# Attention and expert layer on one core: the first block's scores moved ahead, and one step's weight loads made to wait

## The chip, the core and the metric

The kernel runs on one core of one Trainium2 chip. The metric is device microseconds of one execution; the median of three runs before the change is 530.3 us (529.27 to 530.62). The engines go by their names in the profile: PE is TensorE (PEld its weight loads), DVE is VectorE, ACT is ScalarE, POOL is GpSimd, SP is SyncE, which issues most transfers.

## The reference

Two layers follow each other. The first is attention over q, k, v of shape (4, 8, 768, 64): 4 batches, 8 heads, 768 positions, 64 wide. A position sees the 96 positions up to itself and the first 8 of its batch; a distance bias with a slope per head is added, then come softmax and the product with v.

```python
scores = scale * np.matmul(q, k.transpose(0, 1, 3, 2)) + bias
scores = np.where(is_global | is_local, scores, -1e9)
a = softmax(scores); x = (a @ v)            # rows of x: 3072 x 512
```

The second is a layer of 8 experts on the 3072 rows of x. Each row goes to the expert with the largest logit (`x @ w_gate`), and takes the next free slot of that expert (at most 768, in the order of the rows). Each expert computes `relu(rows @ w1) @ w2` with w1 of 512 x 1024 and w2 of 1024 x 512, and the result, times the gate's probability, is the output row.

## The kernel before, in words

**Attention (`banded`).** The 3072 rows are 24 blocks of 128 positions. For block i, `load(i)` (L474) issues three loads of 256 KB on SP: q, k and v (tiles nat_q, nat_k, nat_v), each in pieces of 256 bytes. `prep_k(i)` and `prep_q(i)` turn K and Q on PE, four transposes each into one of the four banks bankA (L511), and copy them out with DVE (K, L524) and ACT (Q, L537). `scores(u)` and `maxima(u)`, where u counts half blocks of four heads, write the scores to two banks of bankA (PE, L564) and add the bias and take the maxima (DVE, L545); `exps(u)` is the exponential on ACT (L575); `transpose_p` turns the probabilities (PE, L593 and L600), `weigh` multiplies them with V (PE, L621 and L624). The loop over t (from L649 on) interleaves the steps of several blocks: in round t it issues the loads of block t + 2 and the window of V, turns the probabilities of block t - 1, prepares K and Q of block t + 1, and then writes the scores of block t. From the end of the setup on, the order on PE, ACT and DVE is the written order; inside the loop that of SP and POOL too.

The two first blocks are loaded ahead of the loop. There V of block 0 and all three loads of block 1 wait until K of block 0 has landed (L483 to L485). Ahead of the loop PE turns Q and K of block 0 and runs six filling matmuls (L74).

**The seam.** Each block of x is stored to a tensor in memory (xrows, L180, on SP) and its rows are routed: logits, expert, slot. The slots go to a table in memory by indirect writes of POOL (L293). Expert 0 starts before all is routed: its slots 0 to 255 are gathered early, and the numbers of the rows in its slots 256 to 511 are worked out from the last blocks (tile gif, L389); `xs[3]()` (L1046) gathers these two blocks of 128 rows from xrows by indirect reads on POOL (L362; the second of them is `got`). They can start when the last block of x (xr_last, L178, L180) has landed in memory. Then POOL writes the last three columns of the table (L293), SP reads the whole table back (tile raw, L840), PE turns it (`turn_slots`, L854, L855), and its row numbers (gi, L1103) drive the gathers of the next expert.

**The experts.** Per expert 8 blocks of 128 columns of w1 (f = 0 to 7), two to a step; there are 32 steps. `raw_weights` (L117) loads a step in four pieces of 256 KB on SP (L134): two of w1 into tiles wr (4 buffers), two of w2 into w2r (7 buffers). Each piece is later split into a high part (ACT, L147) and a rest (DVE, L148), for the products L982 (layer 1) and L990 to L992 (layer 2). Steps 0 to 2 are loaded and split during attention. Step 3 is fetched at L1034, ahead of the gather, and split at f = 2 and 3 of expert 0; step 4 is fetched at f = 2, and so on two steps ahead. Three loads of 512 KB of w2 (L1065) wait for the read of the table. In this stage the order on PE, ACT and DVE is the written one; that of SP and POOL is set by the planner, which goes by written order and by when it reckons that an instruction is ready, so a load may be issued far ahead of its place in the text.

Of the kernel before, what the change touches and what calls it, by code (L numbers as in the profile page):

```python
# [20 lines left out]
P = 128  # L21
# [6 lines left out]
def fused(ctx: ExitStack, tc, q, k, v, wg, w1, w2, out, n_global, n_local, cap):  # L28
    nc = tc.nc
    B, H, S, D = q.shape  # L30
# [33 lines left out]
    SYNC = mybir.DependencyInfo(mybir.DependencyClass.Sync, mybir.DependencyReason.DATA)  # L64
# [26 lines left out]
    for n in range(2):  # L91
        nc.scalar.dma_start(out=wg_sb[n * D:(n + 1) * D, :, n * ER:n * ER + E],
                            in_=wg.rearrange("(c n p) e -> n p c e", n=2, p=D)[n])
# [68 lines left out]
    NBLK = N // P  # L162
    xts, rss = {}, {}
    PREFETCH = 3
# [6 lines left out]
    def store_rows(i):  # L171
        xt = xts[i // 3]
        xr_ps = bankA([P, DM])
        for c in range(KC):
            nc.tensor.transpose(xr_ps[:, c * P:(c + 1) * P], xt[:, c, i % 3, :], ident)

        xr = rt.tile([P, DM], F32, name="xr_last", bufs=1) if i == NBLK - 1 else small.tile([P, DM], F32, name="xr")
        nc.vector.tensor_tensor(xr.rearrange("p (h d) -> p h d", h=H), xr_ps.rearrange("p (h d) -> p h d", h=H),  # L178
                                rss[i // 3][:, i % 3, :].unsqueeze(2).to_broadcast([P, H, D]), op=ALU.mult)
        nc.sync.dma_start(out=xrows[i * P:(i + 1) * P, :], in_=xr)  # L180
# [118 lines left out]
    first = {}  # L299
# [91 lines left out]
    def route_steps(i0, T):  # L391

        r = dict(i0=i0, T=T)
        early = i0 + T < NBLK - LATE
        r["by"] = nc.gpsimd if early else nc.vector

        def s(r, then=None):
            route_p(r)
            route_s(r, then)
            route_g(r)  # L400

        def write(r):
            for i in range(T):
                route_w(r, i)
            if i0 + T == NBLK - EARLIER:
                route_early()
            if i0 + T == NBLK - LATE:
                route_first()

        if i0 + T == NBLK:  # L410

            first["n"] = lambda ps: route_n(r, ps)
            first["s"] = lambda ps, meanwhile: s(r, lambda: route_at(r, ps, meanwhile))
            first["w"] = lambda was=first["w"]: was() + [route_w(r, 0)]
            steps = (route_z, route_l, route_m, route_f)
        elif early:
            steps = (route_z, route_l, route_m, route_f, route_n, route_p, route_s, route_g, write)
        else:
            then = (lambda: route_at(r)) if i0 >= NBLK - LATE else None
            steps = [route_z, route_l, route_m, route_f, route_n, lambda r: s(r, then)]  # L420
            if then:

                first["w"] = lambda: [route_w(r, i) for i in range(T)]
            else:
                steps.append(write)
        return [lambda f=f: f(r) for f in steps]


    def banded():
# [44 lines left out]
        def load(i):  # L474
            b, j = blocks[i]
            d = st_[i]
            for n, src in (("q", q), ("k", k), ("v", v)):
                d[n] = nat.tile([P, H * D], F32, name="nat_" + n, bufs=5 if n == "v" else 3)
                ld = nc.sync.dma_start(out=d[n].rearrange("p (h d) -> p h d", h=H),
                                       in_=src[b, :, j * P:(j + 1) * P, :].rearrange("h p d -> p h d"))  # L480

                if i == 0 and n == "k":
                    first["k"] = ld  # L483
                elif i == 1 or n == "v" and i == 0:
                    tc.add_manual_dep(ld.ins, first["k"].ins.name, SYNC)  # L485

        load(0)
        load(1)
# [6 lines left out]
        def load_window(i):  # L495

            b, j = blocks[i]
            d = st_[i]
            if j == 0:
                d["vg"] = vpool.tile([G, H * D], F32, name="vg")  # L500
                nc.sync.dma_start(out=d["vg"], in_=d["v"][0:G])
            else:
                d["vg"] = st_[i - 1]["vg"]
                d["v1"] = vpool.tile([PREV + G, H * D], F32, name="v1", bufs=3)
                nc.sync.dma_start(out=d["v1"][0:PREV], in_=st_[i - 1]["v"][P - PREV:P])
                nc.sync.dma_start(out=d["v1"][PREV:PREV + G], in_=d["vg"])
# [60 lines left out]
        def exps(u):  # L567
            un = units[u]
            w, sc = un["w"], un["sc"]
            i, half = divmod(u, 2)  # L570
            if half == 0:
                st_[i]["sm"] = small.tile([P, H], F32, name="sm", bufs=3)
            sm = st_[i]["sm"][:, 4 * half:4 * half + 4]
            for a in range(4):
                un["e"] = nc.scalar.activation(sc[:, a, 0:w], sc[:, a, 0:w], AF.Exp, bias=un["mx"][:, a:a + 1], scale=-1.0,  # L575
                                               accum_out=sm[:, a:a + 1])
# [50 lines left out]
        def keep_x(i, by=None):  # L627
            if i % 3 == 0:
                xts[i // 3] = small.tile([P, KC, 3, P], F32, name="xt")
            if by is None:  # L630
                nc.scalar.copy(xts[i // 3][:, :, i % 3, :], st_[i]["xt_ps"])
            else:
                by.tensor_copy(xts[i // 3][:, :, i % 3, :], st_[i]["xt_ps"])
# [6 lines left out]
        def route(block, *steps):  # L640
            if block in groups:
                if block not in routes:
                    routes[block] = route_steps(*groups[block])
                for n in steps:
                    routes[block][n]()
# [3 lines left out]
        for t in range(NBLK + 1):  # L649
            x = t - 2  # L650
            rows = t > 1 and x < NBLK
            if t + 2 < NBLK:
                load(t + 2)
            if t < NBLK:
                load_window(t)
            route(t - 3, 1)
            if t < NBLK:
                route(t - 4, 3)
                route(t - 5, 7, 8)
            else:  # L660
                keep_x(x, nc.vector)
            if t > 0:
                transpose_p(2 * t - 2)
            if t == NBLK:
                store_rows(x)
            if t == NBLK - 1:
                route(t - 3, 2, 3)
            if rows and t < NBLK:
                keep_x(x)
            if t > 0:  # L670
                sums(t - 1)
            if t + 1 < NBLK:
                prep_k(t + 1)
                prep_q(t + 1)
            if t < NBLK - 1:
                route(t - 4, 4, 5)
            if t > 0:
                transpose_p(2 * t - 1)
            if t == NBLK:
                route(t - 4, 5, 6)  # L680
                start_rows()
                turn_first(0)
            if t == NBLK - 1:
                fetch_early()
                route(t - 3, 4)
            if rows and t < NBLK:
                store_rows(x)

            if t == 6:
                for n in range(PREFETCH):  # L690
                    pieces += raw_weights(n, nat, "wst", 4, loads=loads)
            if 6 <= t < 6 + len(loads):
                loads[t - 6]()
            if 8 <= t < 8 + len(pieces):
                pieces[t - 8](meanwhile=True)
            if t < NBLK:
                for u in (2 * t, 2 * t + 1):
                    scores(u)
                    maxima(u)
                exps(2 * t)  # L700
            route(x, 0)
            if t < NBLK:
                exps(2 * t + 1)
            if t > 0:
                weigh(2 * t - 2)
                weigh(2 * t - 1)
                turn_sums(t - 1)
            if t < NBLK:
                if t < NBLK - 1:
                    route(t - 3, 2)  # L710
                route(t - 4, 6)
            if t == 4:
                numbers()
# [299 lines left out]
    def plain(shape):  # L1013
        return moe.tile(shape, F32, name="w2r", bufs=7)

    def fetch(step, after=()):
        if step < STEPS and step not in wparts:
            pieces[step] = raw_weights(step, moe, "wr", 4, after, plain)
# [12 lines left out]
        if s.stop > SURE * P:  # L1031
            nc.scalar.activation(hr, h[:, SURE * P:], AF.Relu)  # L1032

    fetch(PREFETCH)  # L1034


    EARLY = 3
    START, LATER = slice(0, FIRST * P), slice(FIRST * P, T4)
# [5 lines left out]
        layer1(0, f, h_ps[f], xs[0], xs[1], START, (1,))  # L1044
    first["s"](y_ps[FIXED - 1], lambda: hidden(hs0, 0, START))
    got = xs[3]()  # L1046
    for w in first["w"]():
        tc.add_manual_dep(w.ins, got.ins.name, NOSYNC)
    hidden(hs0, 1, START)
# [13 lines left out]
    for step in range(PREFETCH):  # L1063
        t = wparts[step][1]["r"] = plain([P, FP, DM])
        ld = nc.sync.dma_start(out=t, in_=w2[0, step * FP * P:(step + 1) * FP * P, :].rearrange("(f p) d -> p f d", p=P))  # L1065
# [3 lines left out]
    for e in range(E):  # L1069
# [7 lines left out]
        for f in range(NF):  # L1077
# [11 lines left out]
            h = h_ps[f % 2]  # L1089
# [138 lines left out]
```

## Time and profile before

| | |
|---|---|
| median of the runs | 530.3 us (529.27 to 530.62) |
| profiled execution | 527.6 us, of it 525.8 us span |
| mean granted TensorE clock | 0.978 of full |
| PE busy | 488.0 us, 93% of the span |
| DVE busy | 313.2 us, 60% |
| ACT busy | 303.8 us, 58% |
| POOL busy | 130.0 us, 25% |
| DMA | 81.16 MB moved, mean 154 GB/s |

The times of the views below are microseconds from the span's start. In a row of the time-ordered view the first two numbers are the start and the duration; "x4" is the number of instructions merged in it, and the bracket at the end is how long the engine stood idle before it and what ended that. The attention loop runs to about 190 us, the seam from there to about 220 us, the experts from there on.

### The profile page before, as it was taken

To read this page: it belongs to the slowest core of one execution; us is meant where nothing else is said; L and a number is where in the kernel's file an instruction comes from. 1 tells how busy PE (TensorE), PEld (TensorE's weight loads), DVE (VectorE), ACT (ScalarE), POOL (GpSimd) and SP (SyncE) were. 2 spreads that over 40 slices of the span, in tenths; PEclk is the share of its full clock that TensorE was granted. 3 is DMA by queue.
4 is the path that set the end of the run, shared out by engine and by line. 5 is a ranking of instruction groups with operands and counts; after the bars stand their busy time and mean duration, and the time that the engine had idled before them with its cause. 6 is when DMAs were issued, how large, how long until landed. Compare 5 with 4: busy or idle time off the path is not lost.

```text
span 525.8 us, 10453 instructions
## 1 busy us (share of the span) xinstructions
PE 488.0 (93%) x3471; PEld 414.1 (79%) x3471; DVE 313.2 (60%) x945; ACT 303.8 (58%) x813; POOL 130.0 (25%) x222
## 2 busy tenths in 40 slices
PE   6999999999999975999999999999999999999860
PEld 3788888878888764878888889988989988888640
DVE  3777887877888854354546555654655554555320
ACT  1787788887988730344545555545555545546330
POOL 5111334435252322331311321311323103002020
PEclk9999999999999989999999999999999999999995
DMA  8987699989996216295535554563655355332010
GB/s 156 184 190 164 145 212 172 241 168 249 192 169 177 84 36 175 91 371 175 193 105 185 188 152 147 209 178 102 203 176 183 121 164 170 100 97 94 4 38 14
DMA packets 115936, 81.16 MB, mean 154 GB/s; under 512 B 81669, under 2 KB 98085, under 8 KB 115816
## 3 DMA queue, kind: packets, MB, share of 16 engines
q1 hardware_dynamic: 109240, 64.67, 48.2%
q0 software_dynamic: 5888, 14.71, 8.5%
q8 instruction: 88, 1.44, 1.2%
q14 instruction: 32, 0.26, 0.2%
q10 hardware_dynamic: 688, 0.07, 0.1%
HBM read 62.45 MB, written 14.75 MB: 147 GB/s over the span
## 4 chain that ended last, share of the span: by engine, by line
issue 52%; POOL 9%; POOLq 0%
POOL xg L362 5%; POOL out_dram L891 4%; POOL table L293 1%; POOLq L362 0%; POOLq L891 0%; POOLq L293 0%; POOLq L1155 0%
## 5 line engine op out<-in xcount | busy, mean ns | idle before, releaser
L575 ACT ACTIVATE sc<-sc,mx 128x232 f32<-128x232 f32 (+1 forms) x192 | 88.3, 462 | 26.2 <-DVE mx L545 16.8
L982 PE MATMUL bankB<-xh,w1h 128*128 128x416 f32 (+5 forms) x268 | 90.8, 344 | 2.1 <-ACT hr L1032 1.2
L982 PE MATMUL bankB<-xh,w1l 128*128 128x416 f32 (+5 forms) x268 | 89.8, 340 | 0.8 <-issue 0.8
L1029 ACT ACTIVATE hh<-bankB 128x512 fp32r<-128x512 f32 (+1 forms) x67 | 38.8, 580 | 86.8 <-PE bankB L982 80.6
L1030 DVE SCALAR_TENSOR_TENSOR hl<-bankB,hh 128x512 fp32r<-128x512 f32 (+1 forms) x67 | 44.6, 666 | 68.6 <-ACT hh L1029 64.3
L990 PE MATMUL bankA<-w2h,hh 128*128 128x512 f32 x192 | 79.3, 413 | 0.2 <-issue 0.2
L992 PE MATMUL bankA<-w2h,hl 128*128 128x512 f32 x192 | 76.2, 397 | 0.0
L991 PE MATMUL bankA<-w2l,hh 128*128 128x512 f32 x192 | 76.0, 396 | 0.0
L545 DVE CUSTOM_DVE_ANT_0 sc<-bankA,bias 128x232 f32<-128x232 f32 (+1 forms) x192 | 60.0, 377 | 9.4 <-PE bankA L564 9.1
L982 PEld LDWEIGHTS bankB<-xh,w1h 128*128 128x128 f32 x268 | 51.3, 191 | 10.4 <-issue 6.5
L982 PE MATMUL bankB<-xl,w1h 128*128 128x416 f32 (+5 forms) x268 | 57.4, 336 | 0.0
L362 POOL DMA_INDIRECT xg<-xrows,gi x28 | 28.6, 1020 | 111.7 <-PE bankC L347 102.3
L982 PEld LDWEIGHTS bankB<-xh,w1l 128*128 128x128 f32 x268 | 51.3, 192 | 4.1 <-issue 1.4
L148 DVE TENSOR_TENSOR w1l<-wr,w1h 128x512 fp32r<-128x512 f32 x58 | 37.5, 688 | 27.8 <-ACT w1h L147 23.0
L1032 ACT ACTIVATE hr<-bankB 128x256 f32<-128x256 f32 x64 | 24.6, 385 | 49.9 <-DVE hl L1030 44.5
L148 DVE TENSOR_TENSOR w2l<-w2r,w2h 128x512 fp32r<-128x512 f32 x58 | 37.4, 687 | 19.2 <-ACT w2h L147 17.3
L982 PEld LDWEIGHTS bankB<-xl,w1h 128*128 128x128 f32 x268 | 47.0, 188 | 0.7
L891 POOL DMA_INDIRECT out_dram<-ysb,to x16 | 16.0, 998 | 123.5 <-ACT ysb L883 121.1
L564 PE MATMUL bankA<-K,Q 64*128 64x232 f32 (+1 forms) x384 | 45.8, 366 | 0.2 <-DVE xr L178 0.2
L990 PEld LDWEIGHTS bankA<-w2h,hh 128*128 128x128 f32 x192 | 36.3, 189 | 10.3 <-issue 4.5
L992 PEld LDWEIGHTS bankA<-w2h,hl 128*128 128x128 f32 x192 | 36.2, 188 | 8.7
L564 PEld LDWEIGHTS bankA<-K,Q 64*128 64x128 f32 x384 | 36.9, 192 | 5.2 <-issue 3.0
(180 smaller groups left out, 858.9 us busy)
## 6 DMA issues: line engine op xcount, KB each, us to landing
wr<-in_moe_w_dram SPq DMA_DIRECT2D x58, 256.0 KB
w2r<-in_moe_w_dram SPq DMA_DIRECT2D x58, 256.0 KB
nat_q<-in_q_dram SPq DMA_DIRECT2D x24, 256.0 KB
nat_k<-in_k_dram SPq DMA_DIRECT2D x24, 256.0 KB
nat_v<-in_v_dram SPq DMA_DIRECT2D x24, 256.0 KB
xrows<-xr SPq DMA_DIRECT2D x23, 256.0 KB
v<-nat_v SPq DMA_DIRECT2D x20, 192.0 KB
wst<-in_moe_w_dram SPq DMA_DIRECT2D x12, 256.0 KB
```

Of the source, the lines that this page charges most:

```text
L148: (nc.gpsimd if meanwhile else nc.vector).tensor_tensor(parts["l"][:, s], r, parts["h"].bitcast(F32)[:, s], op=ALU.subtract)
L362: ld = nc.gpsimd.indirect_dma_start(out=xg, out_offset=None, in_=xrows[0:n], in_offset=bass.IndirectOffsetOnAxis(ap=gi.bitcast(U32), axis= ...
L545: nc.vector.tensor_tensor_reduce(out=un["sc"][:, a, 0:un["w"]], in0=un["ps"][hh][:, gg, :], in1=un["bias"][:, 4 * (u % 2) + a, :], scale=1 ...
L564: nc.tensor.matmul(pss[hh][:, gg, :], d["qt"][rows, g, :], keys[i // KT][rows, g, o + W - w:o + W], start=True, stop=True)
L575: un["e"] = nc.scalar.activation(sc[:, a, 0:w], sc[:, a, 0:w], AF.Exp, bias=un["mx"][:, a:a + 1], scale=-1.0, accum_out=sm[:, a:a + 1])
L891: w = nc.gpsimd.indirect_dma_start(out=out, out_offset=bass.IndirectOffsetOnAxis(ap=rows.bitcast(U32)[:, 0:1], axis=0), in_=ysb, in_offset ...
L982: nc.tensor.matmul(h_ps[:, s], ww[:, c, fs], xx[:, c, s], start=n == 0, stop=n == 3 * KC - 1)
L990: nc.tensor.matmul(y, hh[:, t], w2h[:, fi], start=f == 0, stop=False)
L991: nc.tensor.matmul(y, hh[:, t], w2l[:, fi], start=False, stop=False)
L992: nc.tensor.matmul(y, hl[:, t], w2h[:, fi], start=False, stop=f == NF - 1)
L1029: nc.scalar.activation(hh[:, s], h[:, s], AF.Relu)
L1030: nc.vector.scalar_tensor_tensor(hl[:, s], h[:, s], 0.0, hh.bitcast(F32)[:, s], op0=ALU.max, op1=ALU.subtract)
```

## The change

Two things are changed. In attention the loads of the two first blocks no longer wait for the first K, and in round 0 the transposes of block 1's K and Q stand behind the scores, maxima and first exponentials of block 0, ahead of its second exponentials; all later rounds are as before. At the seam the fetch of step 3's weights stands behind the gather, and each of its four loads waits until the second gathered block has landed. `fetch(step, after)` hands `after` to `raw_weights`, which adds a wait to each load.

```diff
             for n, src in (("q", q), ("k", k), ("v", v)):
                 d[n] = nat.tile([P, H * D], F32, name="nat_" + n, bufs=5 if n == "v" else 3)
-                ld = nc.sync.dma_start(out=d[n].rearrange("p (h d) -> p h d", h=H),
-                                       in_=src[b, :, j * P:(j + 1) * P, :].rearrange("h p d -> p h d"))
-
-                if i == 0 and n == "k":
-                    first["k"] = ld
-                elif i == 1 or n == "v" and i == 0:
-                    tc.add_manual_dep(ld.ins, first["k"].ins.name, SYNC)
+                nc.sync.dma_start(out=d[n].rearrange("p (h d) -> p h d", h=H),
+                                  in_=src[b, :, j * P:(j + 1) * P, :].rearrange("h p d -> p h d"))
...
-            if t + 1 < NBLK:
+            if 0 < t < NBLK - 1:
                 prep_k(t + 1)
                 prep_q(t + 1)
...
                 exps(2 * t)
+            if t == 0:
+
+                prep_k(1)
+                prep_q(1)
             route(x, 0)
...
-    fetch(PREFETCH)
-
...
     got = xs[3]()
+
+    fetch(PREFETCH, (got,))
     for w in first["w"]():
```

## Rows read from the trace of the kernel before

**Rows 1.** Busy time by stretches: stretch, its length, engines, PEclk, DMA share, GB/s.
```profile
57.00:168.00 111.00, 108.48 (x1165) 93.35 (x1161) 91.56 (x392) 93.37 (x321) 43.30 (x88) 1.00 0.94 198
213.00:500.00 287.00, 284.65 (x1482) 245.24 (x1481) 152.30 (x257) 150.33 (x297) 56.39 (x56) 1.00 0.48 156
```

**Rows 2.** In order of time, TensorE, the first 17 us.
```profile
5.48 0.66 PE L511 MATMUL bankA<-ident,nat_k 128*128 128x128 f32 x4 [0.41 <-DMA nat_k<-in_k_dram]
...
11.12 1.04 PE L511 MATMUL bankA<-ident,nat_k 128*128 128x128 f32 x4 [3.69 <-DMA nat_k<-in_k_dram]
...
12.94 1.97 PE L564 MATMUL bankA<-K,Q 64*128 64x128 f32 x16
...
16.40 0.60 PE L511 MATMUL bankA<-ident,nat_k 128*128 128x128 f32 x4
```

**Rows 3.** In order of time, SyncE's issues, the first load behind the wait.
```profile
5.45 0.37 SPq L479 DMA_DIRECT2D nat_v<-in_v_dram  x1
```

**Rows 4.** Busy time by stretches, the start.
```profile
5.00:6.50 1.50, 1.09 (x8) 0.78 (x8) 1.36 (x6) 0.60 (x1) 1.26 (x5) 1.00 0.00 0
...
11.50:14.50 3.00, 3.00 (x22) 2.67 (x22) 0.99 (x4) 0.60 (x1) 0.00 (x0) 0.50 1.38 218
```

**Rows 5.** In order of time, SyncE's issues around the seam.
```profile
185.55 0.33 SPq L180 DMA_DIRECT2D xrows<-xr  x1
...
196.21 0.38 SPq L325 DMA_DIRECT2D tbf<-table  x1
196.90 0.90 SPq L134 DMA_DIRECT2D wr<-in_moe_w_dram  x2
...
199.30 0.47 SPq L180 DMA_DIRECT2D xrows<-xr_last  x1
199.80 0.43 SPq L134 DMA_DIRECT2D wr<-in_moe_w_dram  x1
216.00 0.73 SPq L840 DMA_DIRECT2D raw<-table  x1
...
221.38 3.52 SPq L134 DMA_DIRECT2D w2r<-in_moe_w_dram  x6
```

**Rows 6.** In order of time, GpSimd around the seam.
```profile
190.39 0.98 POOL L293 DMA_INDIRECT table<-pay,slot_of  x1 [0.30 <-issue]
...
206.24 1.05 POOL L362 DMA_INDIRECT xg<-xrows,gif  x1 [14.87 <-issue]
207.60 1.01 POOL L362 DMA_INDIRECT xg<-xrows,gif  x1 [0.31 <-issue]
...
211.56 0.97 POOL L293 DMA_INDIRECT table<-pay,slot_of  x1 [0.30 <-issue]
```

**Rows 7.** In order of time, VectorE, TensorE and ScalarE at the seam.
```profile
197.28 0.68 DVE L178 TENSOR_TENSOR xr_last<-bankA,rs_last 128x512 f32<-128x512 f32 x1
...
200.27 0.16 DVE L389 TENSOR_TENSOR gif<-bankA,was 128x2 int32<-128x2 f32 x1
...
209.66 1.12 PE L347 MATMUL bankA<-ident,xg 128*128 128x128 f32 x4 [5.04 <-DMA xg<-xrows,gif]
...
218.92 0.21 DVE L850 CAST token<-raw 32x128 f32<-32x128 int32 x1 [1.43 <-DMA raw<-table]
...
219.39 0.25 PE L854 MATMUL bankC<-ident,token 32*128 32x32 f32 x1
...
220.79 1.13 ACT L147 CAST w1h<-wr 128x512 fp32r<-128x512 f32 x2
```

**Rows 8.** Busy time by stretches, around the seam.
```profile
186.00:187.50 1.50, 1.50 (x22) 0.92 (x22) 1.36 (x11) 1.25 (x3) 0.00 (x0) 1.00 0.46 175
192.50:195.50 3.00, 3.00 (x18) 2.90 (x18) 0.44 (x1) 0.01 (x1) 0.00 (x0) 0.50 0.00 0
198.50:204.50 6.00, 5.23 (x36) 4.03 (x34) 4.25 (x30) 0.98 (x3) 0.00 (x0) 1.00 0.95 299
```

**Rows 9.** In order of time, TensorE after the wait at the end of attention.
```profile
191.18 0.43 PE L196 MATMUL bankC<-xt,wg_sb 128*32 128x128 f32 x8 [1.31 <-issue]
```

## The prediction

> **What bounds the kernel now.** I read the busy table by stretches first. Between 57 and 168 us TensorE is busy 108.5 of 111 us at full clock, and between 213 and 500 us 284.7 of 287 us [rows 1]. So the body of both stages is a chain on TensorE, and time is to be had only where that engine stands still. The waits by engine and the time-ordered view then show two holes that belong to this change. The first is at the start: TensorE stands for 3.69 us until the second block's K has landed at 11.12 us, and the first block's scores, whose own K landed at 5.48 us, are queued behind those transposes and start at 12.94 us [rows 2]. The second is at the seam between attention and experts: 5.04 us until the gathered rows land at 209.66 us [rows 7], because the gather itself starts only at 206.24 us [rows 6], though its indices were ready at 200.43 us [rows 7]. The rest of the path moves along with these holes: what is gained there is gained at the end, if no other supply is late.
>
> **Part 1, the start: loads at once.** Before, V of the first block and all of the second wait for the first K: the next load after the first K is issued at 5.45 us, as that K lands [rows 3]. The DMA engines moved nothing between 5.0 and 6.5 us [rows 4]: that is the hole in the supply. Without the wait the stream runs on. Its rate for these loads is 218 GB/s [rows 4], so one load of 262 KB takes 1.2 us. Before, the stream restarts at about 6.6 us; the second block's K is its third load, 6.6 + 3.6 = 10.2 us, and it was seen at 11.12 us, 0.9 us after its data. After, the stream goes on from about 4.8 us, the end of the first K. The third block's K is the sixth load from there: 4.8 + 6 x 1.2 + 0.9 = 12.9 us. I take 12.8 us.
>
> **Part 2, the start: scores first.** Nothing is added or removed: sixteen matmuls go ahead of eight transposes on TensorE, and on ScalarE the second block's Q copy goes between the two halves of exponentials. TensorE is free at 11.12 - 3.69 = 7.43 us [rows 2], and the first block's scores can start there, 5.5 us earlier than 12.94. The moved transposes need the second block's K, by the same sum at 4.8 + 3.6 + 0.9 = 9.3 us, when the scores are nearly over; they fall into the time in which TensorE waits for exponentials, which is their cover. Without that cover they would cost their own 1.2 us (two groups of 0.6 us, by the row at 16.40 us [rows 2]). What is late next? Before, 16.40 - 12.94 = 3.46 us passed from the scores to the third block's transposes; after, that gives 7.43 + 3.46 = 10.9 us, with the moved transposes at most 12.1 us. The third K at 12.8 us is later than both. So the gain is read at the third block's transposes: 16.40 - 12.8 = 3.6 us. Bounds: 5.5 us, if the third K is in time; and 0.5 us, if the six loads are served in turn rather than one after the other, so that the first K lands at about 4.8 + 4.8 + 0.9 = 10.5 us and the scores start some 2 us (5.48 to 7.43 [rows 2]) later, at 12.5 us. I stay with 3.6 us, since the second K landed after barely more than its own three loads had moved although four more were issued behind it.
>
> The wait for the third K leaves TensorE idle for about 1 to 2 us near 11 to 12.8 us. [...] By the rows a slow stretch of 3.0 us does the work of 1.5 us, so with it the sum would be 1.5 us smaller; without it, as below. I leave it out of the sum, for the transposes of the probabilities lie inside this wait, and keep it in the range.
>
> **Part 3, the seam: step 3's weights wait.** Before, four loads of step 3 and two of step 4, 256 KB each, are issued from 196.90 to 199.80 us; the store of the last rows of x is issued at 199.30 us as the sixth of seven [rows 5], though its data were ready at 197.28 + 0.68 = 197.96 us [rows 7]. The seven moved together at 299 GB/s until about 204.5 us [rows 8], and the gather started 1.74 us after that [rows 6]. After, step 3's loads are queued behind the gather's landing. Step 4's take their buffers from the same ring of four after step 3's, so I expect them behind as well. The store then goes at about 198.05 us. An undisturbed store of the same size, issued at 185.55 us [rows 5], had moved its data by 187.5 us [rows 8], so 1.95 us. Gather start: 198.05 + 1.95 + 1.74 = 201.7 us, against 206.24: 4.5 us. It cannot be earlier than the indices, 200.43 us, which bounds the term at 5.8 us.
>
> From the gather's start to the first use there are 3.42 us (206.24 to 209.66), so the rows land at 205.1 us, and of the 5.04 us wait some 0.5 us are left. What is late next is the slot table: two gathers and three scatters run one after another on GpSimd (206.24 to 211.56 + 0.97 us [rows 6]), the table is read at 216.00 us [rows 5], 3.47 us after the last scatter, and VectorE has it at 218.92 us [rows 7]. That is 12.68 us from the gather's start, all of it carried along: 201.7 + 12.7 = 214.4 us. TensorE turns the table 0.47 us later (219.39 [rows 7]), so it cannot gain more than 4.5 us there, however early its rows were.
>
> What the new wait holds: SyncE issues in order, and behind step 3's loads stand step 4's and the read of the table. The second gather lands at about 201.7 + 1.36 + 3.42 = 206.5 us (it starts 207.60 - 206.24 = 1.36 us after the first [rows 6]); six loads are 1.57 MB, at 299 GB/s 5.3 us, so their data run from about 207.7 to 213 us. The table read, due at 211.5 us, can stand up to 1.5 us behind them; with only step 3's four loads (3.5 us, until 211.2) it would not. The scatters can be slower as well: the three that ended at 191.37 us were read only at 196.21 us, 4.84 us [rows 5, 6], against 3.47. I take 0.5 us off. The weights themselves: ScalarE converts the first of them at 220.79 us [rows 7], so at about 216.8 us after; they land by 214 us. That slack of 2.8 us hides the delayed load; beyond it every us is paid. So this part gives 4.0 us, bounds 2.6 (the scatter's 1.4 us more and 0.5) and 5.8.
>
> [...]
>
> **Sum.** 3.6 + 4.0 = 7.6 us. The profiled execution took 527.6 us, a span of 525.8 and 1.8 us around it: 520.0 us after. The median of the three runs is 530.3 us, 2.7 us above it, and the forecast is for such a median: 522.7 us.
>
> **Rivals.**
> (a) The head start is given back in the attention stage, because that is paced by DMA. For it: the engines' share is 0.94 between 57 and 168 us at 198 GB/s [rows 1]. Against it: the saturated stream at the start shows a share of 1.38 [rows 4], and TensorE idles only 2.5 us of the 111. Only the seam is left: 530.3 - 4.0 = 526.3 us.
> (b) The seam does not move: step 4's loads, which wait for nothing new, or others are issued ahead of the store, or the gather waits for something else (the trace puts its wait down to no single transfer for certain). 530.3 - 3.6 = 526.7 us.
> (c) Both: no change, 530.3 us.
> (d) Slower: the order on SyncE puts step 3's loads behind the table read, the three loads of 512 KB that follow it and six more of 256 KB. For it: in the old order the six are issued together behind the table read, at 221.38 us [rows 5]; against it: the gather lands before the scatters. Then 3.1 MB at 299 GB/s, 10.5 us, and 1.8 us for the first half of step 3 pass after the table at 214.9 us, and the first conversion starts at about 228 us instead of 216.8: 11.3 us late, 3.7 us more than is gained, 534.0 us. It decides from a landing after 216.8 + 7.6 = 224.4 us.
>
> **How the numbers follow.** Forecast 0.62; (a) 0.11; (b) 0.12; (c) 0.09; (d) 0.06. About 0.3%, 1.6 us, is what a measurement of this kernel can tell from no change. The forecast, (a) and (b) are faster: 0.85; same 0.09; slower 0.06. The forecast's own bounds: both upper terms nearly (5 and 5.5) give 519.8 us; lower terms (3.6 less 1.5, and 2.6) give 525.6 us. The range goes from 519.5 to 526.8 us, so that it takes in (a) and (b).
>
> **What would show it.** Right: the scores of the first block near 7.5 to 8 us; the third block's transposes near 12.8 us, waiting for K; no load of weights between 196 and 206 us (times of the seam as they stand above; the head start of 3.6 us comes off them as well); the store issued right behind its VectorE instruction; the gather 4 to 5 us closer to the indices; TensorE's wait for the rows under 1 us, and a small new one before the turning of the table. Wrong: the first K later than 7 us; a clock of 0.50 near 13 us; loads of step 4 ahead of the store; ScalarE standing before the first conversion of step 3; a difference at the seam's start that is not kept at 168 us.

## The result and the profile after

The changed kernel takes 525.38 us (median of 8 runs, 522.82 to 526.97) against 529.27 us for the kernel before in the same series: ratio 0.990, 95% interval 0.9875 to 0.9925. By the medians that is 3.9 us, by the ratio 5.3 us. The forecast was 522.7 us and 7.6 us: side and range are right, the gain is a third to a half smaller, and 522.7 / 530.3 = 0.986 lies outside the interval. On another chip the ratio was 0.992 (c_after below).

The profiled execution after took 526.28 us, with a span of 524.6 us (before: 527.6 and 525.8). TensorE is busy for 490.3 us of it, before for 488.0. Three views show the change. First the table by stretches (columns as in [rows 1]): from 11 to 13 us TensorE does next to nothing, from 13 to 16.5 us it runs at 0.53 of its full clock, and from 206 to 214 us the DMA engines are loading (share 0.63, 194 GB/s). The third line lies behind the last rows of x: there the clock is low as well, at 0.50, where it was at 1.00 before [rows 8].

```profile
11.00:13.00 2.00, 0.07 (x2) 0.04 (x1) 0.77 (x2) 1.73 (x9) 0.19 (x1) 1.00 1.36 217
13.00:16.50 3.50, 3.50 (x18) 3.08 (x20) 1.38 (x2) 0.60 (x1) 0.07 (x1) 0.53 1.34 222
198.50:204.20 5.70, 5.70 (x20) 5.02 (x21) 2.80 (x16) 0.38 (x1) 3.78 (x4) 0.50 0.31 92
206.00:214.00 8.00, 7.68 (x52) 6.59 (x50) 2.24 (x4) 2.99 (x7) 0.00 (x0) 1.00 0.63 194
```

Then the view in order of time: start, duration, engine, line and operation, in brackets the idle time before it and its releaser. The shifted line numbers: L506 turns K and Q, L559 is the scores, L839 the read of the slot table, L849 the token, L853 its turning.

```profile
7.95 1.16 PE L559 MATMUL bankA<-K,Q 64*128 64x128 f32 x16
...
12.99 0.92 PE L506 MATMUL bankA<-ident,nat_k 128*128 128x128 f32 x4 [1.93 <-DMA nat_k<-in_k_dram]
...
15.55 2.34 PE L559 MATMUL bankA<-K,Q 64*128 64x232 f32 x16
...
196.20 0.32 SPq L180 DMA_DIRECT2D xrows<-xr_last  x1
...
199.50 1.05 POOL L362 DMA_INDIRECT xg<-xrows,gif  x1 [9.70 <-DVE pay L283]
...
204.61 0.90 SPq L134 DMA_DIRECT2D wr<-in_moe_w_dram  x2
...
204.82 0.97 POOL L293 DMA_INDIRECT table<-pay,slot_of  x1 [0.30 <-issue]
...
205.36 0.60 PE L347 MATMUL bankA<-ident,xg 128*128 128x128 f32 x4
...
206.53 1.32 SPq L134 DMA_DIRECT2D wr<-in_moe_w_dram  x2
...
212.62 0.73 SPq L839 DMA_DIRECT2D raw<-table  x1
...
215.19 0.21 DVE L849 CAST token<-raw 32x128 f32<-32x128 int32 x1 [3.44 <-DMA raw<-table]
...
215.83 0.24 PE L853 MATMUL bankC<-ident,token 32*128 32x32 f32 x1 [2.14 <-DVE gate L851]
...
222.49 0.50 PE L989 MATMUL bankA<-w2h,hh 128*128 128x512 f32 x1 [1.81 <-ACT hr L1031]
```

Against [rows 2, 5 to 7]: the first scores start 5 us earlier, the third block's transposes 16.40 - 12.99 = 3.4 us. The store is issued right behind its data, the gather starts 6.7 us earlier, and TensorE's 5.04 us wait for the rows is gone. But the last table write ends at 204.82 + 0.97 = 205.79 us and the table is read only at 212.62 us: 6.83 us where it was 3.47. Into that gap fall the six loads, issued from 204.61 to 207.85 us. Two new waits of TensorE follow, 2.14 and 1.81 us.

The same milestones, read from the time-ordered view of every profile (starts in us; "write" is the end of the last table write, "last" the scores of the last block):

| profile | 2nd scores | 5th | last | xr_last | gather | write | raw | token | span |
|---|---|---|---|---|---|---|---|---|---|
| before | 18.03 | 39.26 | 179.51 | 197.28 | 206.24 | 212.53 | 216.00 | 218.92 | 525.8 |
| after | 15.55 | 37.22 | 177.96 | 195.49 | 199.50 | 205.79 | 212.62 | 215.19 | 524.6 |
| e_start | 14.57 | 35.74 | 174.40 | 189.30 | 199.81 | 206.10 | 209.54 | 212.02 | 520.6 |
| e_seam | 18.07 | 39.30 | 176.42 | 191.31 | 197.17 | 203.46 | 210.16 | 212.75 | 522.2 |
| e_late | 14.42 | 35.58 | 172.99 | 187.88 | 193.60 | 199.89 | 203.01 | 205.81 | 518.3 |
| e_warm | 14.64 | 35.80 | 174.77 | 189.66 | 195.03 | 201.31 | 208.14 | 211.51 | 521.7 |
| c_before | 17.24 | 38.46 | 176.31 | 192.60 | 202.13 | 208.41 | 211.57 | 214.15 | 522.0 |
| c_after | 15.77 | 37.24 | 177.10 | 194.25 | 198.26 | 204.56 | 211.08 | 213.29 | 520.7 |
| e_queue | 14.24 | 35.42 | 175.50 | 191.74 | 195.76 | 202.04 | 205.47 | 207.71 | 514.5 |
| e_behind | 15.42 | 36.99 | 177.14 | 195.66 | 199.67 | 205.97 | 209.84 | 212.34 | 519.7 |
| e_vlate | 12.59 | 34.15 | 173.93 | 190.21 | 194.22 | 200.51 | 206.66 | 208.91 | 518.0 |
| e_best | 12.64 | 33.81 | 174.97 | 192.14 | 196.16 | 202.46 | 206.15 | 208.31 | 518.0 |
| e_best2 | 13.27 | 34.44 | 174.04 | 190.27 | 194.86 | 201.13 | 205.02 | 207.26 | 516.0 |
| e_last | 12.85 | 34.02 | 172.89 | 189.98 | 194.54 | 200.83 | 204.29 | 206.92 | 513.5 |

The first two rows are from one chip, e_start to e_warm from a second, c_before to e_behind and e_last from a third, e_vlate to e_best2 from a fourth; absolute times are compared within a chip, differences within a profile across them.

### The profile page after: what moved, and what is told of

The parts are those of the page before. It is cut to its first block, busy times and chain, and to the rows that moved or that the text cites. A ratio compares the mean times of both kernels' runs of the same rounds, so it can differ in the third digit from the quotient of the medians.

```text
span 524.6 us, 10457 instructions
## 1 busy us (share of the span) xinstructions
PE 490.3 (93%) x3471; PEld 415.9 (79%) x3471; DVE 313.6 (60%) x945; ACT 304.1 (58%) x813; POOL 129.9 (25%) x222
## 4 chain that ended last, share of the span: by engine, by line
issue 51%; PE 24%; POOL 9%; DMA 7%; ACT 3%; SPq 2%; DVE 1%; POOLq 0%; DVEq 0%; ACTq 0%
PE bankA L559 6%; POOL xg L362 4%; DMA nat_k<-in_k_dram 4%; POOL out_dram L890 4%; PE bankB L588 4%; PE bankA L506 3%; PE bankC L616 3%; PE bankB L595 3%; PE bankC L619 3%; ACT sc L570 2%; DMA v<-vg 2%; SPq L479 1%; PE bankA L175 1%; DMA xg<-xrows,gi 1%; POOL table L293 1%
## 5 line engine op out<-in xcount | busy, mean ns | idle before, releaser
L559 PE MATMUL bankA<-K,Q 64*128 64x232 f32 (+1 forms) x384 | 46.1, 364 | 0.2
L559 PEld LDWEIGHTS bankA<-K,Q 64*128 64x128 f32 x384 | 36.5, 188 | 6.1 <-issue 3.4
```

The costliest lines, as they stand in the source:

```text
L559: nc.tensor.matmul(pss[hh][:, gg, :], d["qt"][rows, g, :], keys[i // KT][rows, g, o + W - w:o + W], start=True, stop=True)
```

## Experiments

**The parts alone, the loads behind the table, and a warm clock.** e_start has the start's part only, e_seam the seam's part only:

```
 e_start = after     +    fetch(PREFETCH)                # back ahead of EARLY = 3
                     -    fetch(PREFETCH, (got,))
 e_seam  = before    -    fetch(PREFETCH)
                     +    fetch(PREFETCH, (got,))        # behind got = xs[3]()
 e_late  = after     -    fetch(PREFETCH, (got,))
                     +    fetch(PREFETCH, (listed,))     # behind raw, listed = slots([got])
 e_warm  = after     +    if t == 1: busy(8)             # ahead of prep_k(2): eight dummy matmuls
```

> The start alone is changed; step 3's weights are fetched ahead of the gather as in the kernel before. Theory (the head start is cut to 1.8 us by the half clock between 13.0 and 16.5 us, and what is left is kept): third block's transposes near 13.0 us, the last rows of x (VectorE, xr_last) near 195.5 us against 197.28, the wait for the gathered rows again about 5 us, the time 1.8 us under the kernel before. Rival, the term as predicted: 3.6 us under it. Rival, attention is paced by DMA: xr_last at 197.3 us and no gain.

> The seam alone is changed; the start is that of the kernel before. Theory (the waiting weights delay the last scatter and TensorE's code, so that of the 4.9 us by which the gather moves some 1.9 us are left): xr_last at 197.3 us, gather start 4.0 us behind it, table on VectorE 19.7 us behind it against 21.6, time 1.9 us under the kernel before. Rival, the term as predicted: table 17.6 us behind it, time 4.0 us under.

> As the changed kernel, but step 3's weights wait until the slot table has been read, so that nothing is loaded beside the scatters and the table. Theory (those loads held the last scatter and TensorE's code back): table read 3.5 to 4 us after the last scatter against 6.8, table on VectorE 16.7 us behind xr_last against 19.7, the long branch of 4.9 us on TensorE under 3 us, time about 2 to 3 us under the changed kernel, if the later weights don't stop ScalarE at their first conversion (then less by that wait). Rival (the scatters land late for themselves, as the three ahead of the early table did, 4.8 us): table read 4.8 us or more after the last scatter, time within 1 us of the changed kernel.

> As the changed kernel, with eight filling matmuls on TensorE in its wait for the third block's K (11.0 to 13.0 us). Theory (half clock after that wait costs 1.6 us of the head start): granted clock 1.00 from 13.0 to 16.5 us, the second block's scores near 14.3 us against 15.55, xr_last 1.2 to 1.6 us earlier than 195.5, time 1.2 to 1.6 us under the changed kernel unless the seam eats it. Rival (the stretch is paced by VectorE and ScalarE): scores earlier, but xr_last at 195.5 us.

Measured against the kernel before (525.69 us): e_start 521.51 us, ratio 0.9913 [0.9888, 0.9939]; e_seam 522.60, 0.9941 [0.9913, 0.9969]; e_late 518.81, 0.9846 [0.9801, 0.9891]; e_warm 524.90, 0.9985 [0.9958, 1.0011]. In e_seam the read of the table, 6.70 us behind the last write, reproduces the delay without any change of the start:

```profile
202.37 0.90 SPq L134 DMA_DIRECT2D wr<-in_moe_w_dram  x2
...
202.49 0.97 POOL L293 DMA_INDIRECT table<-pay,slot_of  x1 [0.30 <-issue]
...
210.16 0.73 SPq L840 DMA_DIRECT2D raw<-table  x1
```

By the medians e_start is 4.2 us under the kernel before, nearer to its rival (3.6) than to its theory (1.8), and e_seam 3.1 us (theory 1.9, rival 4.0).

In e_late, where the loads are issued 2.8 us behind that read, it is 3.12 us, and VectorE has the token 17.9 us after xr_last instead of 19.7 (after), 21.4 (e_seam) or 21.9 (e_warm). A part of these distances comes from the store: in e_seam, e_late and e_warm SyncE issued it 2.1 to 2.4 us after xr_last, behind the read of an earlier table (tbf) that waits for table writes, against 0.71 us in the profile after, and the gather started 5.4 to 5.9 us after xr_last and not 4.0. So the token came later than was expected in e_seam (19.7) and e_late (16.7); with the old seam on this chip (e_start) it came 22.7 us after. The other half of the theory was a branch on TensorE's sequencer ahead of the turning of the table, which took 4.92 us after, from 210.9 to 215.8 us. In e_seam and e_warm, which have the late read too, TensorE's wait there (2.3 and 4.39 us) ended with VectorE's token, and in e_late none stands there; so in the two the read and not the branch set it.

What e_late gained is in part given back at once: ScalarE now waits for the weights, the last time 5.39 us. The two loads that this conversion needs were issued at 210.71 us, ahead of six loads of w2r and behind three of 512 KB, and were not there before 223.06 us.

```profile
198.92 0.97 POOL L293 DMA_INDIRECT table<-pay,slot_of  x1 [0.30 <-issue]
...
203.01 0.73 SPq L839 DMA_DIRECT2D raw<-table  x1
205.80 2.13 SPq L134 DMA_DIRECT2D wr<-in_moe_w_dram  x2
...
209.23 0.62 ACT L147 CAST w1h<-wr 128x512 fp32r<-128x512 f32 x1 [1.58 <-DMA wr<-in_moe_w_dram]
...
210.71 1.05 SPq L134 DMA_DIRECT2D wr<-in_moe_w_dram  x2
211.80 10.52 SPq L134 DMA_DIRECT2D w2r<-in_moe_w_dram  x6
...
223.06 1.36 ACT L147 CAST w1h<-wr 128x512 fp32r<-128x512 f32 x2 [5.39 <-DMA wr<-in_moe_w_dram]
```

The clock. e_start waits as long for the third K as the changed kernel does, 2.11 us, and yet its clock stays up: second scores at 14.57 us, 1.0 us earlier than after. e_warm fills the wait (0.39 us left) and the clock is at 1.00 from 13 to 16.5 us, but its fifth block is no earlier than e_start's. So beside e_start there was nothing to save, and e_warm is slower than e_start alone (its interval only touches that of e_seam). Its profile shows the same late read (6.83 us), a longer wait of TensorE for the token (4.39 us) and a mean clock of 0.66 from 210 to 220 us; but e_start has 0.68 from 200 to 210 us at the seam too. Why e_warm is that much slower stays open. The first two lines are e_start's, the others e_warm's:

```profile
13.14 0.63 PE L506 MATMUL bankA<-ident,nat_k 128*128 128x128 f32 x4 [2.11 <-DMA nat_k<-in_k_dram]
13.00:16.50 3.50, 3.36 (x31) 2.92 (x32) 2.12 (x7) 0.90 (x2) 0.10 (x1) 1.00 1.35 222
...
11.00:13.00 2.00, 1.82 (x9) 0.62 (x7) 0.79 (x2) 1.82 (x9) 0.09 (x1) 1.00 1.37 219
13.00:16.50 3.50, 3.29 (x30) 2.85 (x32) 2.06 (x7) 0.83 (x2) 0.16 (x1) 1.00 1.34 219
```

**Both kernels again, and two other places for the loads.** e_queue puts them behind the table's read in the queue without waiting until it has landed; e_behind puts them ahead of gather and writes:

```
 e_queue:  -    fetch(PREFETCH, (got,))
           +    fetch(PREFETCH, (listed,), NOSYNC)        # behind slots([got]); order only
 e_behind: -    fetch(PREFETCH, (got,))
           +    fetch(PREFETCH, (first["st"],), NOSYNC)   # order behind the store of xr_last
```

> The changed kernel itself, beside the next ones. Theory (the weights held back run beside the third scatter and hold it up): raw is read 6.5 to 7 us after the last scatter has ended, as in e_seam and e_warm, the token comes 21 to 22 us after xr_last, and the ratio to the kernel before is 0.990 to 0.995. Rival (the two parts simply add): 0.9913 of e_start and 0.9941 of e_seam multiply to 0.9855, raw is read 3.5 us after the last scatter.

> The kernel before, profiled on this chip: raw 3.5 us after the last scatter, the gather 8 to 9 us after xr_last, the token 21.6 us after it (all as in its first profile); time 525 to 529 us.

> As e_late, but step 3's loads stand right behind the read of the slot table in SyncE's queue and don't wait until it has landed (205.80 - 203.01 = 2.8 us earlier). If a transfer that is first in its queue keeps its place: the token comes 17.9 us after xr_last as in e_late, ScalarE's waits of 1.58 + 1.34 us for the weights go, and the ratio is 0.981 to 0.984. If loads hold up any small transfer near them, as they did the third scatter: the token comes 2 to 3.5 us later (20 to 21.4 after xr_last), and the ratio is 0.988 to 0.992.

> Step 3's and step 4's loads stand right behind the store of the last rows in SyncE's queue, ahead of gather and scatters; the store is as early as in the changed kernel. Six loads of 256 KB take 5.3 us at 299 GB/s, so they are done about 9.7 us after xr_last; the last scatter starts 11 us after it (e_late). If only what runs beside loads is late: gathered rows 2 to 3.4 us late (TensorE waits 2 to 5 us for them), the scatter not, raw 3.1 to 3.5 us after it, the token 18 to 19 us after xr_last, ratio 0.984 to 0.988. If the gather's delay is passed on through GpSimd's order: the token at 20 to 21.4 us, ratio 0.990 to 0.994, so no better than the changed kernel.

Against 525.78 us: c_after 521.06 us, 0.9920 [0.9888, 0.9952]; e_queue 518.26, 0.9872 [0.9826, 0.9919]; e_behind 519.58, 0.9888 [0.9836, 0.9941]; c_before's one profiled run took 523.79 us. The timings do not separate the three (their intervals overlap, and e_queue's ratio lies above its forecast of 0.981 to 0.984); the profiles do. Write to read: 3.16 us in c_before, 6.52 in c_after, 3.43 in e_queue, 3.87 in e_behind. xr_last to token: 21.6, 19.0, 16.0 and 16.7 us. In e_queue the loads stand 0.8 us behind the read and do not hold it up, so the harm is not done to any small transfer near them, but to the table write that goes out together with them:

```profile
201.07 0.97 POOL L293 DMA_INDIRECT table<-pay,slot_of  x1 [0.30 <-issue]
...
205.47 0.73 SPq L839 DMA_DIRECT2D raw<-table  x1
206.25 0.95 SPq L134 DMA_DIRECT2D wr<-in_moe_w_dram  x2
...
207.71 0.22 DVE L849 CAST token<-raw 32x128 f32<-32x128 int32 x1 [0.97 <-DMA raw<-table]
```

In e_behind it is the gather that runs beside the loads, and the rows come 204.97 - 199.67 = 5.30 us after its start instead of the 3.42 us of the kernel before [rows 6, 7]; the writes start when GpSimd has issued the gathers, so only TensorE waits, 1.97 us:

```profile
199.67 1.06 POOL L364 DMA_INDIRECT xg<-xrows,gif  x1 [10.70 <-DVE pay L285]
...
204.97 0.66 PE L349 MATMUL bankA<-ident,xg 128*128 128x128 f32 x4 [1.97 <-DMA xg<-xrows,gif]
...
209.84 0.73 SPq L841 DMA_DIRECT2D raw<-table  x1
```

c_after and e_behind fell to the low clock, 0.51 and 0.53, behind the wait for the third K, c_after thus:

```profile
13.00:16.50 3.50, 3.46 (x16) 3.11 (x18) 1.31 (x2) 0.60 (x1) 0.00 (x0) 0.51 1.35 221
```

e_queue, with the same start, did not (1.00 from 13 to 16.5 us, second scores at 14.24 against 15.77 us). With the profile after, e_start and e_late that makes three profiles of six in which the clock fell behind a wait of 1.8 to 2.1 us. What decides it was not found.

**The wait for the third K taken away, and the pieces put together.** e_vlate loads Q and K of the third block ahead of all V; e_best is that with e_queue; e_best2 also puts the read of an earlier table (tbf), which waits for table writes, behind the store of xr_last on SyncE; e_last also has five buffers for w2r:

```
 e_vlate: -  load(0); load(1)
          +  load(0, "qk"); load(1, "qk")
          +  # t == 0: load(2, "qk"), then V of blocks 0, 1 and 2
 e_best2: +  store_rows(NBLK - 1)
          +  first["read"]()              # tbf's load, with its old waits
 e_last:  -  name="w2r", bufs=7
          +  name="w2r", bufs=5
```

> The changed kernel with V of the first two blocks loaded behind Q and K of the third: the third K is the sixth load and not the eighth, 2 x 1.2 us earlier. If TensorE's wait for that K costs the head start: third K near 10.6 us instead of 12.8 to 13.0, no wait over 0.5 us before it, granted clock 1.00 throughout 10 to 20 us, scores of the second block at 12.2 to 12.8 us (14.2 at full clock, 15.4 to 15.8 at half clock in the runs so far), those of the fifth at 33.4 to 34 us (35.4 to 37.2 so far); seam as in the changed kernel (raw 6.5 us after the last scatter); ratio 0.985 to 0.990. If the stream of loads paces attention anyway: the wait comes back as one for V or for the fourth K, the fifth block's scores stay at 35.4 us or later, ratio 0.990 to 0.994.

> e_queue with the order of loads of e_vlate. If both causes are the right ones: start as in e_vlate, token 16 to 18 us after xr_last, ratio 0.979 to 0.984. If only the seam's: 0.985 to 0.988, as e_queue.

> e_best with the read of the first table queued behind the store of the last rows and not ahead of it. Where attention ends early, that read stands before the store and waits for the last table write (store 2.36 us after xr_last in e_late, 0.71 us in e_queue). If the store's place counts: 0.71 us in any case, and up to 1.6 us less than e_best where e_best shows a later store; otherwise the same as e_best within 1 us.

> e_best2 with five buffers and not seven for the second layer's raw weights, so that of the six loads that stand ahead of the fifth step's first-layer weights in SyncE's queue four come later. Theory (what was gained at the token is partly given back where ScalarE waits for those weights: 2.30 us in e_best2, 1.75 in e_best, 5.39 in e_late): the wait at the second pair of conversions goes, they start near 218 us instead of 220.5, and from the token to the end of the span there are 306 to 307 us instead of 308.7; ratio 0.979 to 0.983. Rival (TensorE has slack there, or fewer buffers make a later load late): 308 us or more from the token to the end, ratio 0.983 to 0.990.

Against 526.15 us: e_vlate 519.58 us, 0.9878 [0.9842, 0.9914]; e_best 519.38, 0.9863 [0.9832, 0.9894]; e_best2 517.40, 0.9843 [0.9798, 0.9888]. e_last, against 526.71 us: 517.07, 0.9816 [0.9774, 0.9858]. In e_vlate the wait is gone and the clock stays up; the one that comes in its place, for the fourth K, is 0.75 us:

```profile
10.44 0.60 PE L506 MATMUL bankA<-ident,nat_k 128*128 128x128 f32 x4
...
12.59 1.84 PE L559 MATMUL bankA<-K,Q 64*128 64x232 f32 x16
...
17.79 0.63 PE L506 MATMUL bankA<-ident,nat_k 128*128 128x128 f32 x4 [0.75 <-DMA nat_k<-in_k_dram]
```

The clock was 1.00 from 11 to 16.5 us in e_vlate and e_last; the second block's scores took 1.84 us in all four kernels with that order, as in e_warm at 1.00, against 2.34 us after, and their fifth block starts at 33.8 to 34.4 us. At the seam e_vlate still has the late read (6.15 us) and the other three don't (3.46 to 3.89). In time that can't be told apart here: e_best, with its token 16.2 us after xr_last instead of 18.7, stands at 0.9863 beside e_vlate's 0.9878, above the 0.979 to 0.984 that were expected if both causes count. So the late read is shown at the table, and what it is worth in the whole time is not. e_best2 could not show the store's place: the store is issued 0.7 us after xr_last in e_best as well, since attention ended late enough on that chip, and the 0.002 between the two is not explained.

In e_last there are 306.6 us from token to end as expected (e_best2: 308.7), but ScalarE's wait went only from 2.30 to 1.61 us. The expectation had taken the wrong loads for the ones that ScalarE waits for: those that moved forward, to 212.65 us (in e_best2 220.57), are the next step's and are converted at 230.53 us. The conversion that waits needs the pair before, issued at 209.94 us (in e_best2 210.21), ahead of the loads of w2r in both kernels. So the shorter time from token to end has another cause than the one given, or is within the scatter of single profiles:

```profile
209.94 1.57 SPq L134 DMA_DIRECT2D wr<-in_moe_w_dram  x2
...
212.65 2.35 SPq L134 DMA_DIRECT2D wr<-in_moe_w_dram  x2
...
219.93 1.39 ACT L147 CAST w1h<-wr 128x512 fp32r<-128x512 f32 x2 [1.61 <-DMA wr<-in_moe_w_dram]
...
230.53 1.13 ACT L147 CAST w1h<-wr 128x512 fp32r<-128x512 f32 x2
```

e_last is below the changed kernel: beside c_after on the same chip the intervals do not overlap. From e_best2, measured on another chip, it is not separated.

## Why the prediction was right in part

*Bounds and parts 1 and 2.* The holes were where the rows put them. First scores 7.95 us (forecast 7.5 to 8), third K 12.99 (12.8). The 3.6 us are there where the clock stays up: e_seam to e_start, one with the old start and one with the new, 39.30 - 35.74 = 3.56 us at the fifth block. Where it falls, 39.26 - 37.22 = 2.0 us are left. The sentence that failed is "I leave it out of the sum": the price was right (1.5 us; the fifth block at 37.0 to 37.2 against 35.4 to 35.8 us), but in three profiles of six it was paid. The reason given, that the transposes of the probabilities lie inside this wait, did not hold: they are done 1.9 us before the third K lands. The slow stretch that the 1.5 us were worked out from is that of 3.0 us at 0.50 [rows 4, 8], which came after waits of 3.69 and of 1.31 us [rows 2, 9]; that such a wait brings it was the author's estimate, and behind the wait for the third K the clock was at 0.51 to 0.53 in three profiles of six.

*Rival (a), the head start given back in attention.* A part of it, and on the third chip more. From the fifth to the last block the new start took 0.5 us more than the old one on the first chip (140.74 against 140.25), 0.3 to 1.9 on the second (e_start, e_late and e_warm against e_seam), 2.0 to 2.3 on the third (c_after, e_queue and e_behind against c_before), where c_after was only 1.2 us ahead at the fifth block and is 0.8 us behind c_before at the last. On the second chip the waits name DMA (1.7 us for K in e_start, 1.1 for V in e_warm); on the third they are waits for ScalarE. Against it: e_start is 4.2 us faster than the kernel before. With one profile of the old start on each chip I take the sign as likely and the size as open.

*Part 3, the seam.* Store, order on SyncE, gather and the vanished wait came as worked out: from xr_last to the gather 8.96 us before and 4.01 after, 4.95 us gained against 4.5 forecast (5.5 us in c_before and c_after). Step 4's loads did queue behind step 3's, and ScalarE did not wait for the weights. The step that failed is "I take 0.5 us off" for table writes beside loads: it measured 6.83 - 3.47 = 3.4 us (3.4 in c_after as well), and not as a queue ahead of the table's read, but in the last write: SyncE had issued its last load by 207.85 us and then waited 4.6 us for that write. With it the token gains not 4.0 us but 1.9 in its distance from xr_last (2.5 on the third chip). Of the terms that were read it is the largest of the miss, and e_late and e_queue, which take the loads away from the writes, have the token 17.9 and 16.0 us after xr_last, where the kernel before has 21.6 us in both of its profiles. None of the rows shows a table write beside such loads; the 1.5 us at most by which the read was to stand behind them were too few as well.

*Behind the token* the forecast let everything move along. In the profile after, token to end is 309.4 us against 306.9, so 2.5 us are lost there, 1.81 of them in the wait at 222.49 us; in c_after it is 307.4 against 307.8. What makes this wait is open: it is put down to ScalarE's hr, and stands in no other profile; the branch on TensorE's sequencer before it took 4.69 us and ended 1.3 us before the wait did, which was not tested. It is not all of it, since e_seam and e_warm, without that wait, have 309.5 and 310.2 us.

The forecast had no clock at the seam, and there it fell too. From xr_last to the token TensorE is busy 17.32 of 19.70 us after and 15.69 of 21.64 before, so it stands 3.6 us less; but the granted clock of that stretch is 0.83 against 0.92. That makes some 3.4 against 1.7 us of work not done, by my estimate (0.17 x 19.70 and 0.08 x 21.64 us). In c_after and c_before it is the other way: 0.75 from 190 to 198 us and 0.97 from 200 to 212 us, against 1.00 and 0.72, by time 0.88 against 0.83 in the mean. So of the seam's gain in the profile after about 1.6 us went to the clock, and a single pair of profiles does not show whether the change is to blame.

*Open too:* the parts' ratios multiply to 0.9855, the changed kernel stands at 0.990 and 0.992. The delayed write is in e_seam already, so it doesn't explain the difference; the intervals allow additivity only at their edges, and the whole was not timed on the chip of the parts. The two profiles differ by 1.3 us in time where the medians differ by 3.9 (the profiled run before lies 1.7 us under its median, the one after 0.9 above), so terms read from them can't add up to the measured gain. That the forecast's range holds is in part luck: two terms were too large, and what else differs between the runs is not known. Rivals (b) and (c) fell with the gather; (d) with the order on SyncE (its own sum, 214.9 + 10.5 + 1.8, gives 227.2 us and not 228, so its time would have been 533.1 us).

## What to carry to other kernels

Before a bulk load is held back, look at what small transfer will be under way when it is let go: here the loads beside the last table write cost 3.4 of the 5 us by which the gather had come forward, and behind the table's read in the same queue they did not hold that read up. A wait shortened from 3.7 to about 2 us still cost the clock behind it in three profiles of six (0.51 to 0.53). Taking away what it waits for (two loads later in line) left the scores behind it at 1.84 us in four profiles of four; filling it kept the clock at 1.00 too, but that kernel was not faster, for a reason left open. Read a gain at several milestones, not at the end alone: it can be made and given back on the way.

## What the runs showed of the hardware that was not expected

- A small table write that goes out together with 1.57 MB of loads (the first of the six is issued 0.07 to 0.23 us before it): its end was seen some 3 us later, in all five profiles of this kind (after, e_seam, e_warm, c_after, e_vlate: 6.15 to 6.83 us from write to read; in the other nine 3.12 to 3.89). In after, e_seam and c_after SyncE had issued the loads 2.1 us after the write's end, and the read followed 4.4 to 4.8 us later; in e_warm and e_vlate issuing them took longer, and the read followed 1.9 and 2.7 us later. The loads suffer too. The line of DMA traffic after, 40 slices of 0.275 us from 203 us on, shows next to nothing moved from 205.5 until some 208.5 us although their issue began at 204.61 us:

```profile
GB/s 313 313 75 18 0 0 0 3 1 26 11 0 0 0 0 0 0 7 0 0 112 227 387 186 209 291 228 310 220 250 381 380 354 399 391 373 313 320 175 142
```

- The clock is no function of the wait alone: after waits of 1.93, 2.13 and 2.06 us (after, c_after, e_behind) it fell to 0.51 to 0.53, after 2.11, 1.83 and 2.12 us (e_start, e_queue, e_late) it stayed at 1.00, with the same instructions before.
